# Attention, feed-forward and top-1 experts on one core: the gate logits of three token blocks on VectorE instead of TensorE, and two reorderings in block 0

## The chip, the core and the metric

The kernel runs on one core of a Trainium2 chip. The metric is the time of one execution on the device, in microseconds (us). Three executions of the kernel before took 570.47 to 570.69 us, median 570.53.

## What is computed

Three stages follow each other, over 1536 tokens with 512 features:

```python
# 1. attention: 2 sequences x 8 heads x 768 positions x 64; each position sees
#    the first 4 positions and the 128 latest
a = softmax(where(is_sink | in_window, q @ k.T / sqrt(D), -1e9)) ; attn = a @ v
x = attn as (1536, 512)
# 2. feed-forward, 512 -> 2048 -> 512; its weights come as 64-bit floats
h = x @ w_in ; g = maximum(0.01 * h, h) ; x = g @ w_out
# 3. eight experts, each token goes to one
logits = x @ w_gate                         # (1536, 8)
expert_idx = argmax(logits, axis=1) ; gate_w = softmax(logits)[expert_idx]
# a token keeps its place among the first 384 of its expert, in token order
y = maximum(x_of_expert @ w1[e], 0) @ w2[e] # 512 -> 1024 -> 512
out[i] = gate_w[i] * y[i] if kept else 0
```

The result is wanted in 32-bit precision.

## The kernel before

Large products are made from parts of 32-bit numbers: an operand is split in a *high* part (a cast, names `wh`, `xth`, `gp`) and a *low* part (the rest, `wl`, `xtl`), and a product is the sum of high x high, high x low and low x high.

**Blocks.** The feed-forward stage works on six blocks (0 to 5) of 256 tokens, each of two tiles of 128. For a block the 2048 hidden features are done in 16 *column tiles* f of 128: `first` (line 1084) makes `hps`, 12 products of 128x256 over the four slices k of the 512 features; `leak` (1102) applies the leaky maximum, with ScalarE at 1117 and VectorE's `max` at 1118; `split_g` (1121) makes the high half on ScalarE (1127) and the low half on GpSimd (1129); `second` (1132) adds the tile's part to the two outputs `y`, two column tiles later. Between these steps lie the steps of attention for a later block: transposes `qps`, VectorE's `qT` and `kTl` (586, 590), scores `sps` (617), the softmax (626 to 651), the outputs `ops` (713), and the low part of the attention output, `xtl`, in `pv_low` (728, VectorE at 732). Scores and other small TensorE results take turns in the same PSUM buffers.

**Block 0** is written out in `block0()` inside `build`. While it runs, VectorE makes 32-bit weights out of the 64-bit words, three operations of 128x512 for each piece: `low_word`, `sign` and `tail` (1017, 1021, 1027; tiles `word` and `cvt`). A first pass goes through `first` for f = 0 to 15, a second one through `second`. The first column tiles (five in the first pass, ten in the second) take their weights unsplit; from then on ScalarE casts `wh` (1045) and GpSimd subtracts `wl` (1046). The order of every engine is the order in which Python issues the work. A planner, `Pace`, keeps a time for TensorE and one for VectorE by assumed costs; whenever VectorE work is issued through `pace.vector`, `fill` first puts weight words in front of it for as long as the planner thinks that VectorE has time:

```python
    def vector(self, us, wait=0.0):
        self.fill()
        self.dve = max(self.dve, self.pe + wait) + us
```

After block 0 VectorE's order is left to the scheduler; the other engines keep the order written.

**Routing.** The last `second` of block j-1 falls in step 1 of block j's loop (a loop has 16 steps, one per column tile). ScalarE then copies `y` to a token tile (`evac`, 1224), and the routing steps of that block are put in a list, `routing`. After step i of the loop the next of them is issued if i is in `ROUTE`:

```python
ROUTE = (2, 4, 6, 9, 10, 11, 14)
                if routing and i in ROUTE:
                    routing.pop(0)()
```

The steps are: `transpose` (TensorE turns the token tile by eight transposes `xps`, line 1233; VectorE copies `x2T`, 1235), `parts` (sixteen small products `kls`, 1245, one ScalarE copy), `logits` (four products `lps`, 1258; VectorE finds the expert, 1265 to 1279), `place` (each token's row, 1293 to 1315) and two `scatter` (1322, an indirect DMA on GpSimd's queue that writes the tokens to their expert's rows). In block 4's loop `ex.rank` is put before the last of them; it sorts the experts by their counts. So the tokens of blocks 1, 2 and 3 are routed in the loops of blocks 2, 3 and 4. The experts' own products (`craw` and `cw`, 1472 and 1474, are their weights) come behind block 5. SP's queue carries the loads: attention's inputs (`natq`, 175), the weights and more.

Of the kernel before, what the change touches and what calls it, by code (L numbers as in the profile page):

```python
# [8 lines left out]
F32 = mybir.dt.float32  # L9
# [4 lines left out]
ALU = mybir.AluOpType  # L14
# [4 lines left out]
P = 128  # L19
# [14 lines left out]
PAIR = 2  # L34
# [12 lines left out]
AHEAD = (5, 10)  # L47
WORD_US = 0.6
PARTS_US = 2.0
ROUTE = (2, 4, 6, 9, 10, 11, 14)  # L50
HOLD, TAIL = 4, 1
QUIET = 2
# [376 lines left out]
class RingAttention(Attention):  # L429
# [298 lines left out]
    def pv_low(self, t, g):  # L728
        if (t, g) in self.lo:
            lo, hi, ps = self.lo.pop((t, g))  # L730
            self.pace.vector(0.4)
            self.nc.vector.tensor_tensor(out=lo, in0=ps, in1=hi.bitcast(F32), op=ALU.subtract)

    def pipeline(self, ts, n_first, first):
# [216 lines left out]
class FFN:  # L951
# [132 lines left out]
    def first(self, j, f):  # L1084
        nc, N = self.nc, self.N
        pool, tag = ("psy", "y1") if j == 0 and f % 2 else ("psh", "h")
        ps = self.p[pool].tile([P, 512], F32, tag=tag, name="hps")[:, 0:N]
        kc = lambda t: t.rearrange("p (k c) -> p k c", k=self.K)
        if self.in_parts(j, f, 0):
            wh, wl = map(kc, self.w[f][0])  # L1090
            xh, xl = [[x[:, k, :] for k in range(self.K)] for x in self.xt(j)] if j else \
                [[self.x0[k // 2][a][:, k % 2, :] for k in range(self.K)] for a in range(2)]
            mm = ((wh, xh), (wh, xl), (wl, xh))
        else:
            x = self.xt(j)[0]
            mm = ((kc(self.v[f][0]), [x[:, k, :] for k in range(self.K)]),)
        mm = [(w[:, k, :], x[k]) for k in range(self.K) for w, x in mm]
        for n, (w, x) in enumerate(mm):
            nc.tensor.matmul(ps, lhsT=w, rhs=x, start=(n == 0), stop=(n == len(mm) - 1))  # L1099
        self.g[j, f] = ps  # L1100
# [49 lines left out]
class Router:  # L1150


    def __init__(self, nc, tc, pools, A, capacity, ident):
        self.nc, self.tc, self.p, self.A = nc, tc, pools, A
        self.sent, self.both = [], ()
        self.ident = ident
        self.DM, self.E = A["moe2_w_gate"].shape
        self.NTOK = A["out"].shape[0]
        self.cap = max(0, min(int(capacity), self.NTOK))
        self.NU = -(-self.cap // P)  # L1160
        self.rows = self.NU * P
        self.K = self.DM // P
        self.OOB = 1 << 20
        self.KEEP = self.E // 2 - 1
        self.apart = self.NU > 1 and self.E > 1
        self.x2, self.xT, self.st = {}, {}, {}
        c = pools["const"]
        self.tiled = self.K * 32 <= P and self.E <= 32
        wg = c.tile([P, self.K, 32 if self.tiled else self.E], F32, name="wg")
        self.wgp, self.wg = wg, wg[:, :, 0:self.E]  # L1170
        if self.tiled:

            nc.gpsimd.memset(wg, 0.0)
            self.fold = c.tile([P, self.E], F32, name="fold")
            nc.gpsimd.memset(self.fold, 0.0)
            for k in range(self.K):
                nc.gpsimd.affine_select(out=self.fold, in_=self.fold, pattern=[[-1, self.E]],
                                        compare_op=ALU.not_equal, fill=1.0, base=-32 * k, channel_multiplier=1)
        self.lT = {}
        nc.sync.dma_start(out=self.wg, in_=A["moe2_w_gate"].rearrange("(k p) e -> p k e", p=P))  # L1180

        self.before = c.tile([P, P], BF16, name="before")
        nc.gpsimd.memset(self.before, 1.0)
        nc.gpsimd.affine_select(out=self.before, in_=self.before, pattern=[[1, P]], compare_op=ALU.is_gt, fill=0.0,
                                base=0, channel_multiplier=-1)
        self.ones = c.tile([P, P], BF16, name="ones")
        nc.gpsimd.memset(self.ones, 1.0)
        self.rev = c.tile([P, self.E], F32, name="rev")
        self.num = c.tile([P, self.E], F32, name="num")
        self.seat = c.tile([P, self.E], F32, name="seat")  # L1190

        seats, short = [0], list(range((self.E + 1) // 2, self.E))
        for e in range(1, (self.E + 1) // 2):
            seats += [e] + short[:1]
            del short[:1]
        seats += short
        for e in range(self.E):
            nc.gpsimd.memset(self.rev[:, e:e + 1], float(self.E - e))
            nc.gpsimd.memset(self.num[:, e:e + 1], float(e))
            nc.gpsimd.memset(self.seat[:, e:e + 1], float(seats[e]))  # L1200
        self.kept = c.tile([P, self.E], F32, name="kept")
        self.run = c.tile([P, self.E], F32, name="run")
        nc.gpsimd.memset(self.run, 0.0)
        self.tok = c.tile([P, self.NTOK // P], I32, name="tok")
        nc.gpsimd.iota(self.tok, pattern=[[P, self.NTOK // P]], base=0, channel_multiplier=1)

        self.places = pools["dram"].tile([max(1, self.rows * self.E), self.DM + 2], F32, name="places")
        self.queues = self.places[0:self.rows * self.E, :].rearrange("(e r) c -> e r c", e=self.E)
# [19 lines left out]
    def transpose(self, ts):  # L1228
        nc = self.nc
        for t in ts:  # L1230
# [4 lines left out]
            nc.vector.tensor_copy(xT, ps)  # L1235
            self.xT[t] = xT

    def parts(self, ts):

        nc = self.nc  # L1240
        ps = self.p["ps"].tile([32 * self.K, len(ts), P], F32, tag="att", name="kls")
        for n, t in enumerate(ts):
            xT = self.xT.pop(t)
            for k in range(self.K):
                nc.tensor.matmul(ps[32 * k:32 * k + 32, n, :], lhsT=self.wgp[:, k, :], rhs=xT[:, k, :],
                                 start=True, stop=True)
        lT = self.p["c"].tile([32 * self.K, len(ts), P], F32, tag="c", name="lT")
        nc.scalar.copy(lT, ps)
        self.lT[ts] = lT

    def logits(self, ts):
        nc, E, sm = self.nc, self.E, self.p["sm"]
        nt = len(ts)
        ps = self.p["ps"].tile([P, nt, E], F32, tag="att", name="lps")
        lT = self.lT.pop(ts, None)
        for n, t in enumerate(ts):
            if lT is not None:
                nc.tensor.matmul(ps[:, n, :], lhsT=lT[:, n, :], rhs=self.fold[0:32 * self.K, :], start=True, stop=True)
                continue
            xT = self.xT.pop(t)  # L1260
            for k in range(self.K):
                nc.tensor.matmul(ps[:, n, :], lhsT=xT[:, k, :], rhs=self.wg[:, k, :],
                                 start=(k == 0), stop=(k == self.K - 1))
# [4 lines left out]
        for n in range(nt):  # L1268
            nc.vector.scalar_tensor_tensor(out=sc[:, n, :], in0=ps[:, n, :], scalar=m[:, n:n + 1], in1=self.rev,
                                           op0=ALU.is_equal, op1=ALU.mult)  # L1270
# [7 lines left out]
                                op0=ALU.mult, op1=ALU.add)  # L1278
# [666 lines left out]
def build(tc, A, n_sink, window, capacity):  # L1945
    nc = tc.nc
# [3 lines left out]
    ring = RingAttention.fits(n_sink, window)  # L1950
    NTOK, DM = A["out"].shape
    N = FFN.N
    NB = NTOK // N
    TPB = N // P
    p = {}

    def pool(st, name, **kw):
        p[name] = st.enter_context(tc.tile_pool(name=name, **kw))

    with ExitStack() as es:  # L1960

        work, att, rawst, psy, psh, psc, pst = (ExitStack() for _ in range(7))
# [29 lines left out]
        steps, done = [], -1  # L1992
# [97 lines left out]
        rt = None  # L2090
# [13 lines left out]
        if not ring:  # L2104
            ex.PARTS -= FEWER

        pending, held, routing, splits = [], [], [], []
        n_ev = ffn.NF - ffn.CAP
        late = NB - 1

        def route(ts, ahead=False):
            return [lambda: rt.transpose(ts), *[lambda: rt.parts(ts)] * (ahead and rt.tiled), lambda: rt.logits(ts),
                    *[lambda: None] * (ahead and not rt.tiled), lambda: rt.place(ts),
                    *(lambda t=t: rt.scatter(t) for t in ts)]

        def split(n, f=-1, x=0):

# [4 lines left out]
        def second():  # L2122
# [23 lines left out]
            if last:  # L2146
                ts = tuple(range(j * TPB, (j + 1) * TPB))
                for t, y in zip(ts, ffn.y.pop(j)):
                    rt.evac(t, y)
                routing.extend(route(ts, True))  # L2150
                if j == late - 2 and rt.NU:
                    routing.insert(-1, ex.rank)

# [59 lines left out]
        pool(psh, "psh", bufs=2, side="right", space=PSUM)  # L2213
        rawst.close()
        pool(es, "rt", bufs=2)
        for j in range(1, NB):
            need_t = TPB * (j + 2) - 1
            count = next((n + 1 for n, x in enumerate(steps) if x[0] == need_t), len(steps))
            ndone = 0
            early = j == late and rt.NU  # L2220
            if j == late:
                att.close()
            if early:
                pool(es, "mx", bufs=1)
                ex.start_x()
            for i, f in enumerate(ffn.order(j)):
# [18 lines left out]
                    ndone += 1  # L2245
                split(SPLIT)
                some(clears, rate)
                if routing and i in ROUTE:
                    routing.pop(0)()
                if early:  # L2250
                    ex.room = min(ex.RAW + ex.PARTS, 6 + 4 * max(0, i - 1) - (0 if ring else FEWER))
# [84 lines left out]
```

## Time and profile before

| | |
|---|---|
| median of three executions | 570.53 us (570.47 to 570.69) |
| the profiled execution, its own time | 570.18 us |
| its span in the trace | 568.1 us, granted clock 0.998 |
| PE (TensorE) busy | 550.2 us, 97%, 3801 instructions |
| PEld (weight loads of TensorE, beside PE) | 472.4 us, 83% |
| DVE (VectorE) busy | 341.0 us, 60%, 829 instructions |
| ACT (ScalarE) busy | 291.6 us, 51% |
| POOL (GpSimd) busy | 186.4 us, 33% |
| DMA | 91.63 MB, mean 161 GB/s |

The page is of one profiled execution; 570.18 us is its whole time and 568.1 us the stretch from its first to its last recorded instruction. Busy time is an average over the whole program: block 0 ends at about 97 us, blocks 1 to 5 follow at some 60 us each, and the experts fill the rest. In a timeline row the first number is the start, the second how long it took, and brackets hold the idle time in front with what ended it.

### The profile page before, as it was taken

The numbers are of one execution on the slowest core, as the hardware profiler recorded it, in microseconds if no ns is written. First come the engines' busy times: TensorE is split into PE (matmuls) and PEld (weight loads), VectorE is DVE, ScalarE is ACT, GpSimd is POOL, SyncE is SP. The second block draws the span as 40 slices with busy tenths as digits, with TensorE's granted clock in tenths as the row PEclk, the third lists the DMA queues.
The fourth block names the chain that finished last, engine by engine and source line by source line (L and its number), as shares of the span: only waits on it lengthen the run. The fifth ranks groups of instructions, "written<-read, shape, count | busy, mean of one in ns | idle before, by whom it ended". The sixth has DMA issues, their size and how long they took to land.

```text
span 568.1 us, 11287 instructions
## 1 busy us (share of the span) xinstructions
PE 550.2 (97%) x3801; PEld 472.4 (83%) x3801; DVE 341.0 (60%) x829; ACT 291.6 (51%) x859; POOL 186.4 (33%) x338
## 2 busy tenths in 40 slices
PE   8988999999999999999999999999999999999994
PEld 7777657888898888888888888887899898988783
DVE  6999995766443533444444522575577666637992
ACT  6767646765445545444444433453444443526771
POOL 5567679623422243224332322241202011001120
PEclk9999999999999999999999999999999999999999
DMA  9979865999242023402230157562487676437930
GB/s 232 239 230 278 272 217 164 312 254 344 81 125 80 20 75 94 113 20 64 70 99 2 40 159 246 170 208 68 148 263 244 199 221 194 148 120 213 315 104 9
DMA packets 83557, 91.63 MB, mean 161 GB/s; under 512 B 42980, under 2 KB 51172, under 8 KB 83489
## 3 DMA queue, kind: packets, MB, share of 16 engines
q1 hardware_dynamic: 81504, 85.68, 50.3%
q0 software_dynamic: 1984, 5.13, 2.6%
q8 instruction: 32, 0.52, 0.4%
q14 instruction: 37, 0.29, 0.2%
HBM read 72.01 MB, written 20.09 MB: 162 GB/s over the span
## 4 chain that ended last, share of the span: by engine, by line
PE 75%; DVE 8%; issue 6%; DMA 5%; POOL 2%; ACT 2%; SPq 0%; POOLq 0%; DVEq 0%; ACTq 0%
PE hps L1099 21%; PE y L1147 21%; PE ph L1636 10%; PE py L1685 9%; PE ops L713 3%; PE sps L617 2%; DMA craw<-in_moe_w 2%; DMA out<-ys,gt 2%; DVE word L1017 2%; DVE word L1021 2%; PE pps L675 1%; PE qps L564 1%; DMA rawo<-in_moe_w_out 1%; DVE cvt L1027 1%; PE xps L1233 1%
## 5 line engine op out<-in xcount | busy, mean ns | idle before, releaser
L1147 PE MATMUL y<-wh,gp 128*128 128x512 f32 x344 | 126.7, 409 | 0.9 <-ACT gp L1127 0.7
L1129 POOL TENSOR_TENSOR gp<-g,gp 128x256 fp32r<-128x256 f32 x77 | 57.2, 743 | 179.9 <-ACT gp L1127 163.6
L1118 DVE TENSOR_TENSOR g<-hps,g 128x256 f32<-128x256 f32 x80 | 33.7, 422 | 103.6 <-ACT g L1117 101.5
L1099 PE MATMUL hps<-xth,wh 128*128 128x256 f32 x320 | 91.9, 287 | 0.4 <-DVE g L1118 0.4
L1099 PE MATMUL hps<-xtl,wh 128*128 128x256 f32 x320 | 90.2, 282 | 0.0
L1099 PE MATMUL hps<-xth,wl 128*128 128x256 f32 x320 | 89.9, 281 | 0.0
L1474 DVE TENSOR_TENSOR cw<-craw,cw 128x512 fp32r<-128x512 f32 x128 | 83.1, 693 | 10.3 <-ACT cw L1472 8.1
L1147 PEld LDWEIGHTS y<-wh,gp 128*128 128x128 f32 x344 | 64.5, 188 | 16.0 <-ACT gp L1127 1.1
L1472 ACT CAST cw<-craw 128x512 fp32r<-128x512 f32 x112 | 63.3, 621 | 23.7 <-PE py L1685 23.0
L1117 ACT ACTIVATE g<-hps 128x256 f32<-128x256 f32 x80 | 30.6, 382 | 84.6 <-PE hps L1099 80.0
L1147 PE MATMUL y<-wl,gp 128*128 128x512 f32 x172 | 67.6, 393 | 0.0
L1685 PE MATMUL py<-cw,ht 128*128 128x512 f32 x264 | 64.1, 398 | 0.2 <-DVE ht L1673 0.2
L1099 PEld LDWEIGHTS hps<-xth,wh 128*128 128x128 f32 x320 | 60.3, 188 | 4.5 <-DVE g L1118 1.4
L1099 PEld LDWEIGHTS hps<-xtl,wh 128*128 128x128 f32 x320 | 60.2, 188 | 2.1
L1099 PEld LDWEIGHTS hps<-xth,wl 128*128 128x128 f32 x320 | 60.6, 189 | 0.0
L1685 PEld LDWEIGHTS py<-cw,ht 128*128 128x128 f32 x264 | 48.9, 188 | 11.8 <-DVE ht L1673 1.0
L1636 PE MATMUL ph<-xt,cw 128*128 128x256 f32 (+2 forms) x444 | 57.7, 290 | 0.1
L1636 PEld LDWEIGHTS ph<-xt,cw 128*128 128x128 f32 x444 | 56.5, 189 | 0.5 <-issue 0.3
L1694 POOL DMA_INDIRECT out<-ys,gt x11 | 11.1, 1007 | 112.8 <-DVE ys L1693 101.8
L1127 ACT CAST gp<-g 128x256 fp32r<-128x256 f32 x80 | 32.9, 411 | 21.6 <-DVE g L1118 20.2
L640 ACT ACTIVATE pm<-pm,mx 128x132 f32<-128x132 f32 (+1 forms) x80 | 31.9, 402 | 10.3 <-DVE mx L632 10.3
L1147 PEld LDWEIGHTS y<-wl,gp 128*128 128x128 f32 x172 | 32.5, 189 | 4.4 <-POOL wl L1046 0.3
(255 smaller groups left out, 993.1 us busy)
## 6 DMA issues: line engine op xcount, KB each, us to landing
craw<-in_moe_w SPq DMA_DIRECT2D x128, 256.0 KB
rawi<-in_moe_w_in SPq DMA_DIRECT2D x16, 512.0 KB
rawo<-in_moe_w_out SPq DMA_DIRECT2D x16, 512.0 KB
places<-zero SPq DMA_DIRECT2D x24, 257.0 KB
wh<-wscr SPq DMA_DIRECT2D x16, 256.0 KB
wl<-wscr SPq DMA_DIRECT2D x16, 256.0 KB
xg<-places SPq DMA_DIRECT2D x12, 257.0 KB
natv<-in_v SPq DMA_DIRECT2D x12, 256.0 KB
```

The lines of the kernel that those rows point to most:

```text
L640: self.nc.scalar.activation(a, a, AF.Exp, bias=mx[:, pr, e:e + 1], accum_out=su[:, pr, e, 0:1])
L713: nc.tensor.matmul(ps[64 * e:64 * e + 64, pr, :], lhsT=l, rhs=r, start=(x == 0 and not (late and pr)), stop=(x == len(mm[0]) - 1 and not l ...
L1099: nc.tensor.matmul(ps, lhsT=w, rhs=x, start=(n == 0), stop=(n == len(mm) - 1))
L1117: nc.scalar.activation(g, ps, AF.Copy, scale=0.01)
L1118: nc.vector.tensor_tensor(out=g, in0=ps, in1=g, op=ALU.max)
L1127: nc.scalar.copy(gp[:, 0], g)
L1129: eng.tensor_tensor(out=gp[:, 1], in0=g, in1=gp[:, 0].bitcast(F32), op=ALU.subtract)
L1147: nc.tensor.matmul(y, lhsT=l, rhs=r, start=(start and n == 0), stop=(stop and n == len(mm) - 1))
L1472: nc.scalar.copy(h, t)
L1474: eng.tensor_tensor(out=l, in0=t, in1=h.bitcast(F32), op=ALU.subtract)
L1636: nc.tensor.matmul(self.ph[f][:, sl], lhsT=self.w[e, "a", h, k][w][:, f * P:(f + 1) * P], rhs=self.xt[:, a, k, sl], start=(m == 0), stop=( ...
L1685: nc.tensor.matmul(self.py[n], lhsT=x, rhs=w, start=(h == 0 and f == 0 and m == 0), stop=(h == self.NH - 1 and f == self.HF - 1 and m == 2))
```

## The change

1. **Logits of blocks 1, 2 and 3 on VectorE.** At the start of block 2's loop SP issues a load of `rows_of`, the 512x8 gate weights copied to each of the 128 partitions (16 KB each, 2.1 MB). For each token tile and each expert one `scalar_tensor_tensor` multiplies the tile (128x512) by that expert's 512 weights, which lie 8 words apart, and sums each row into the logit: 16 such products for a block. Two are issued after each of eight steps (a list `beside`), 1 to 8. Then `logits` (without its TensorE part), `place` and the two scatters come in steps 9, 10, 11 and 12, `AFTER` in the place of `ROUTE`; with `ex.rank` in block 4's loop it is 12 and 13 for the last two. The transposes, `parts` and the `lps` products of these three blocks are gone. Blocks 0, 4 and 5 are routed as before.
2. **Low weights last in block 0.** In `first` of block 0 the 12 products run high x high for all k, high weight x low token for all k, then low weight x high token, and no longer k by k.
3. **`pv_low` without words in front.** It adds its cost to the planner's time by itself and does not call `fill`.

```diff
+AFTER = range(9, 16)
 ROUTE = (2, 4, 6, 9, 10, 11, 14)
...
     def pv_low(self, t, g):
         if (t, g) in self.lo:
             lo, hi, ps = self.lo.pop((t, g))
-            self.pace.vector(0.4)
+            self.pace.dve = max(self.pace.dve, self.pace.pe) + 0.4
             self.nc.vector.tensor_tensor(out=lo, in0=ps, in1=hi.bitcast(F32), op=ALU.subtract)
...
-        mm = [(w[:, k, :], x[k]) for k in range(self.K) for w, x in mm]
+        mm = [(w[:, k, :], x[k]) for w, x in mm for k in range(self.K)] if j == 0 else \
+            [(w[:, k, :], x[k]) for k in range(self.K) for w, x in mm]
...
+    def start_rows(self):
+
+        self.rows_of = self.p["wgb"].tile([P, self.DM, self.E], F32, name="rows_of")
+        src = self.A["moe2_w_gate"].rearrange("(o d) e -> o (d e)", o=1)
+        self.nc.sync.dma_start(out=self.rows_of.rearrange("p d e -> p (d e)"),
+                               in_=src.to_broadcast([P, self.DM * self.E]))
+
+    def products(self, ts, n, es):
+
+        nc, DM = self.nc, self.DM
+        if ts not in self.lg:
+            self.lg[ts] = self.p["sm"].tile([P, len(ts), self.E], F32, tag="rsc", name="rlg")
+        junk = self.p["c"].tile([P, DM], F32, tag="c", name="junk")
+        for e in es:
+            nc.vector.scalar_tensor_tensor(out=junk, in0=self.x2[ts[n]][:, 0:DM], scalar=1.0,
+                                           in1=self.rows_of[:, :, e], op0=ALU.mult, op1=ALU.mult,
+                                           accum_out=self.lg[ts][:, n, e:e + 1])
...
-        ps = self.p["ps"].tile([P, nt, E], F32, tag="att", name="lps")
+        ps = self.lg.pop(ts, None)
+        done = ps is not None
+        if not done:
+            ps = self.p["ps"].tile([P, nt, E], F32, tag="att", name="lps")
...
-        for n, t in enumerate(ts):
+        for n, t in enumerate(() if done else ts):
...
         def route(ts, ahead=False):
+            if ahead and rt.rows_of is not None and len(ts) == 2:
+                es = list(range(rt.E))
+                beside.extend(lambda n=n, e=e: rt.products(ts, n, es[e:e + PAIR])
+                              for n in range(len(ts)) for e in range(0, rt.E, PAIR))
+                return [lambda: rt.logits(ts), lambda: rt.place(ts), *(lambda t=t: rt.scatter(t) for t in ts)]
...
+        def late_route(ts):
+            rt.rows_of = None
+            return route(ts, True)
...
-                routing.extend(route(ts, True))
+                routing.extend(route(ts, True) if j < late - 1 else late_route(ts))
...
+            if j == 2 < late and ring and rt.tiled and TPB == 2:
+                pool(wgb, "wgb", bufs=1)
+                rt.start_rows()
...
             if j == late:
+                rt.rows_of = None
+                wgb.close()
                 att.close()
...
-                if routing and i in ROUTE:
+                if beside:
+                    beside.pop(0)()
+                elif routing and i in (ROUTE if rt.rows_of is None else AFTER):
                     routing.pop(0)()
```

How VectorE's order changes in steps 1 to 3 of block 2's loop, where the tokens of block 1 are routed (`g` is the leak's maximum, `x_2526` a token tile, `junk` the products themselves, `rlg` their sums). Before:

```order
L1118 TENSOR_TENSOR g<-hps,g 128x256
L648 TENSOR_REDUCE ri<-su_134 128x4
L649 RECIPROCAL ri<-ri 128x4
L1118 TENSOR_TENSOR g<-hps,g 128x256
L586 SCALAR_TENSOR_TENSOR qT<-qps,qT 128x256
L590 TENSOR_TENSOR kTl_130<-qps,kTh_129 128x2x128
L1235 COPY x2T<-xps 128x512 x2
L1118 TENSOR_TENSOR g<-hps,g 128x256
L732 TENSOR_TENSOR xtl<-ops,xth 128x2x128
L533 TENSOR_TENSOR vh<-vsraw,vh 32x256
```

And with the change:

```order
L1120 TENSOR_TENSOR g<-hps,g 128x256
L1255 SCALAR_TENSOR_TENSOR junk,rlg<-x_2526,rows_of 128x512 x2
L649 TENSOR_REDUCE ri<-su_134 128x4
L650 RECIPROCAL ri<-ri 128x4
L1120 TENSOR_TENSOR g<-hps,g 128x256
L587 SCALAR_TENSOR_TENSOR qT<-qps,qT 128x256
L591 TENSOR_TENSOR kTl_130<-qps,kTh_129 128x2x128
L1255 SCALAR_TENSOR_TENSOR junk,rlg<-x_2526,rows_of 128x512
L1120 TENSOR_TENSOR g<-hps,g 128x256
L1255 SCALAR_TENSOR_TENSOR junk,rlg<-x_2526,rows_of 128x512
L733 TENSOR_TENSOR xtl<-ops,xth 128x2x128
L534 TENSOR_TENSOR vh<-vsraw,vh 32x256
```

The products stand between the maxima of the leak and the attention steps, and in front of `xtl`; the two copies of `x2T` are gone.

TensorE in block 0, the sixth column tile, the first whose weights are split (`x0h` and `x0l` are the parts of the tokens). Before:

```order
L1099 MATMUL hps<-xth,cvt 128x256 x8
L1099 MATMUL hps<-x0h,wh 128x256
L1099 MATMUL hps<-x0l,wh 128x256
L1099 MATMUL hps<-x0h,wl 128x256
L1099 MATMUL hps<-x0h,wh 128x256
```

and so on, four times three products, one k after the other.

And with the change:

```order
L1101 MATMUL hps<-xth,cvt 128x256 x8
L1101 MATMUL hps<-x0h,wh 128x256 x4
L1101 MATMUL hps<-x0l,wh 128x256 x4
L1101 MATMUL hps<-x0h,wl 128x256 x4
L565 MATMUL qps<-ident,natq 128x128 x2
```

The first use of `wl` moves from the third place of twelve to the ninth.

VectorE in block 0, around `pv_low` (`xtl`). Before:

```order
L590 TENSOR_TENSOR kTl_130<-qps,kTh_129 128x2x128
L1017 TENSOR_SCALAR word<-rawo 128x512 x2
L732 TENSOR_TENSOR xtl<-ops,xth 128x2x128
L1021 SCALAR_TENSOR_TENSOR word<-rawo,word 128x512
L627 COPY_PREDICATED pm<-sel,sps 128x128 x4
L632 TENSOR_REDUCE mx<-pm 128x4
```

And with the change:

```order
L591 TENSOR_TENSOR kTl_130<-qps,kTh_129 128x2x128
L1018 TENSOR_SCALAR word<-rawo 128x512 x2
L733 TENSOR_TENSOR xtl<-ops,xth 128x2x128
L1022 SCALAR_TENSOR_TENSOR word<-rawo,word 128x512
L628 COPY_PREDICATED pm<-sel,sps 128x128 x4
L633 TENSOR_REDUCE mx<-pm 128x4
```

Nothing moved here but the line numbers, and the rest of VectorE's rows in block 0 are the same too. On GpSimd's queue the scatters move, and SP has one row more, the load of `rows_of` between the loads of `natq` and `natk` and that of `natv`.

## Rows read from the trace of the kernel before

**Rows 1.** Stage table: stretch, length; busy us of engines; PEclk, DMA, GB/s.

```profile
97.00:156.00 59.00, 59.00 (x462) 51.88 (x461) 34.60 (x95) 34.35 (x117) 26.61 (x42) 1.00 0.87 255
165.20:195.70 30.50, 30.50 (x236) 26.45 (x234) 14.19 (x45) 16.59 (x61) 8.79 (x15) 1.00 0.24 62
```

**Rows 2.** Waits (us, times, longest): TensorE, whole; VectorE, 26 to 82.6.

```profile
PE hps L1099 <- POOL wl L1046: 3.6, 5, 0.9
...
DVE word L1017 <- DMA rawo<-in_moe_w_out: 0.5, 1, 0.5
```

**Rows 3.** Timelines near the end of block 0: start, us, engine, line.

```profile
71.98 0.69 DVE L1017 TENSOR_SCALAR word<-rawo 128x512 int32<-128x512 int32 x1 [0.54 <-DMA rawo<-in_moe_w_out]
...
82.73 1.07 POOL L651 TENSOR_TENSOR pm<-pm,ri 128x528 f32<-128x528 f32 x1 [2.48 <-DVE ri L649]
...
95.20 0.74 POOL L1129 TENSOR_TENSOR gp<-gr,gp 128x256 fp32r<-128x256 f32 x1
...
95.99 0.73 PE L1147 MATMUL y<-wh,gp 128*128 128x512 f32 x2 [0.19 <-POOL gp L1129]
```

**Rows 4.** Timeline of TensorE in block 2's loop.

```profile
168.26 0.39 PE L1147 MATMUL y<-wh,gp 128*128 128x512 f32 x1
168.49 1.04 PE L1233 MATMUL xps<-ident,x 128*128 128x128 f32 x8
169.49 0.28 PE L1099 MATMUL hps<-xtl,wh 128*128 128x256 f32 x1
...
172.73 0.39 PE L1147 MATMUL y<-wh,gp 128*128 128x512 f32 x1
173.07 0.28 PE L1099 MATMUL hps<-xtl,wh 128*128 128x256 f32 x1
...
176.66 0.39 PE L1147 MATMUL y<-wh,gp 128*128 128x512 f32 x1
176.98 0.64 PE L1245 MATMUL kls<-x2T,wg 128*32 128x128 f32 x16
177.77 0.28 PE L1099 MATMUL hps<-xtl,wh 128*128 128x256 f32 x1
...
183.93 0.39 PE L1147 MATMUL y<-wh,gp 128*128 128x512 f32 x1
184.16 0.51 PE L1258 MATMUL lps<-fold,lT 128*128 128x8 f32 x4
184.72 0.28 PE L1099 MATMUL hps<-xtl,wh 128*128 128x256 f32 x1
```

**Rows 5.** Groups by shape: busy us, mean ns of one, idle before.

```profile
L1235 DVE COPY x2T<-xps 128x512 f32<-128x512 f32 x12 | 7.8, 685 | 4.2 <-PE xps L1233 4.2
L1046 DVE TENSOR_TENSOR wl<-cvt,wh 128x512 fp32r<-128x512 f32 x10 | 8.5, 846 | 3.8 <-ACT wh L1045 3.7
L1338 DVE TENSOR_REDUCE kept<-sel 128x8 f32<-128x24 f32 x1 | 0.2, 181 | 0.0
L1306 DVE TENSOR_REDUCE rpp<-rpos 128x2 f32<-128x16 f32 x5 | 0.8, 169 | 0.0
L1354 DVE TENSOR_REDUCE rank<-gt 128x8 f32<-128x64 f32 x2 | 0.4, 210 | 0.0
L640 ACT ACTIVATION_READ_ACCUMULATOR pm<-pm,mx 128x1 f32 x80 | 15.4, 192 | 0.0
L1021 DVE SCALAR_TENSOR_TENSOR cvt<-rawo,cvt 128x512 int32<-128x512 int32 x1 | 1.4, 1410 | 0.0
```

**Rows 6.** Timelines of VectorE and TensorE, middle of block 2's loop.

```profile
187.22 0.42 DVE L732 TENSOR_TENSOR xtl<-ops,xth 128x256 fp32r<-128x256 f32 x1
189.71 0.40 PE L617 MATMUL sps<-kTh,qT 64*128 64x264 f32 x2
```

**Rows 7.** Timelines of SP's queue and ScalarE.

```profile
148.54 0.52 SPq L175 DMA_DIRECT2D natq<-in_q  x1
...
164.85 1.17 ACT L1224 COPY x<-y 128x512 f32<-128x512 f32 x2
```

**Rows 8.** One tile's instructions: min/median/max ns, first and last start.

```profile
L1472 ACT CAST cw<-craw x112: 608/621/635, 356.6 to 555.5; 128x512 fp32r<-128x512 f32 x112
```

More of the change, by code (lines that the diff above doesn't have):

```diff
@@ L1180, in __init__ @@
         nc.sync.dma_start(out=self.wg, in_=A["moe2_w_gate"].rearrange("(k p) e -> p k e", p=P))
+        self.rows_of, self.lg = None, {}
         self.before = c.tile([P, P], BF16, name="before")
@@ L2105, in build @@
             ex.PARTS -= FEWER
-        pending, held, routing, splits = [], [], [], []
+        pending, held, routing, splits, beside = [], [], [], [], []
         n_ev = ffn.NF - ffn.CAP
@@ L2215, in build @@
         pool(es, "rt", bufs=2)
+        wgb = ExitStack()
         for j in range(1, NB):
+            if j == 2 < late and ring and rt.tiled and TPB == 2:
+                pool(wgb, "wgb", bufs=1)
+                rt.start_rows()
             need_t = TPB * (j + 2) - 1
```

## The prediction, made before the changed kernel ran

> **What bounds the kernel now.** I read the stage table first, then TensorE's waits, then the timelines. From block 1 on TensorE is the bound: it is busy for 59.00 of 59.00 us in block 1 and for 30.50 of 30.50 us in the first half of block 2, at a granted clock of 1.00, while VectorE works 14.19 us of the same 30.50 [rows 1]. There, work taken off TensorE is time, and VectorE has room.
>
> Block 0 is different. TensorE's longest list of waits is there: 3.6 us in five waits for a low weight part [rows 2]. Yet TensorE does not set that block's end. Near it, TensorE stops for a low half from GpSimd, at 95.99, right behind the `gp` that ran 95.20 to 95.94. GpSimd had been working through its queue since 82.73, which it began after an idle 2.48 us, released by `ri` of VectorE. VectorE in turn works through weight words up to that `ri` with one stop, 0.54 us before 71.98, for a DMA [rows 3]; its list of waits from 26 us on has nothing else [rows 2]. So block 0 ends when VectorE's words and GpSimd's splits are through, and a TensorE that is early merely waits at 95.99 instead.
>
> **The change, part by part.** *Removed from TensorE, three times.* I take the distance from the last `y` to the second `hps` behind it. Undisturbed it is 172.73 to 173.07, 0.34. With the eight transposes between it is 168.26 to 169.49, 1.23, so they cost 0.89. With the sixteen small `kls` products it is 176.66 to 177.77, 1.11: 0.77. With the four `lps` it is 183.93 to 184.72, 0.79: 0.45 [rows 4]. Together 2.11 us; all of it is on the path, since TensorE has no gap around it. Three blocks: 3 x 2.11 = 6.3 us gained. ScalarE loses one small copy per block and is not the bound.
>
> *Added to VectorE.* Per block 16 products of 128x512 whose two inputs lie in SBUF, one read in steps of 8 words, each with a sum. No row shows this instruction, so I build its price. The nearest plain form, one operation over 128x512, is 685 ns. The group `wl` of VectorE, with both inputs in SBUF and GpSimd working beside it, takes 846 on average: 0.16 for that company. Steps of 8 words occur in one small row: `kept<-sel`, 24 elements, 181 ns, where a line through 169 for 16 elements and 210 for 64 gives 176. The 5 ns over 24 elements make 0.2 ns each, so 0.10 us for 512. Reading out a sum is a row of 192 ns on ScalarE; VectorE shows none, so I take half, 0.10. That makes 0.69 + 0.16 + 0.10 + 0.10 = 1.05 us. The ends are 0.69, nothing added, and 1.41, the longest single row of this size with two SBUF inputs [rows 5]. I stay near the 846 row, because it has the same two kinds of input, in the same stage.
>
> *Does it fit?* The products are due in steps 1 to 9. TensorE's stretch shrinks to 30.50 - 2.11 = 28.4 us. VectorE's other work there is 14.19 [rows 1] less two copies of 685 ns [rows 5], 12.8. That leaves 15.6 us of room. A late VectorE first meets TensorE at the scores: `xtl` ends at 187.64, the scores that want its PSUM buffer start at 189.71, 2.07 us of slack [rows 6]. (15.6 + 2.07) / 16 = 1.10 us per product is the point from which TensorE waits. At 1.05 nothing shows; beyond 1.10 each tenth costs 1.6 us per block, 4.8 in all, and at 1.10 + 2.11 / 16 = 1.23 the gain is gone. The leak's `max`, which stands between the products on VectorE, has its reader two steps on, further off than the scores. GpSimd's low halves may wait for a product, and their readers are as far off.
>
> *The 2.1 MB of weight rows.* SP issues them right behind the load at 148.54. At the 255 GB/s of block 1 [rows 1] they take 8.2 us and are there at about 158. The first product needs its token tile, which ScalarE copies from 164.85 [rows 7]. Seven microseconds of cover: nothing.
>
> *Moved.* Logits go from steps 4 and 6 to 9, places from 9 to 10, the scatters from steps 10 and 14 to 11 and 12 (13 in block 4): the same instructions on VectorE, TensorE and the GpSimd queue, three steps before the next block wants their buffers. The expert ranking goes from step 11 to 12, one step later; SP waits for it before it asks for expert weights, whose first conversion is at 356.6 [rows 8], half a block on. Nothing.
>
> *Block 0.* With the low weights last, eight of twelve products run before the low part is needed, so most of the 3.6 us goes from that place and comes back at 95.99. The cover is GpSimd's queue; if it went, up to 3.6 us would be gained. I take 0. The edit of `pv_low` changes only the planner's sum: VectorE's order in block 0, shown above, is the same row for row, so no word moves, and it is worth 0 by any account.
>
> **Sum.** The profiled execution took 570.18 us, and 570.18 - 6.3 = 563.9. The median is 0.35 above it, so I say 564.2.
>
> **Rivals.** *VectorE becomes the bound, and the kernel slower.* Mechanism: the step of 8 words slows each product, the backlog reaches `xtl`, and the scores wait for their PSUM buffer in blocks 2, 3 and 4. It decides from 1.23 us per product. At the upper end, 1.41, the wait is 16 x (1.41 - 1.10) = 5.0 us per block, 15 in all, and 570.5 + 15 - 6.3 = 579.2. For it speaks that VectorE is filled to the brim in these steps; against it the 181 ns row, where full one-element steps cost little. [...]
>
> *Block 0 pays as well.* If GpSimd's chain were released by TensorE somewhere, 3.6 us more would go: 560.6. Against it: VectorE's one stop in front of that `ri` is for a DMA and not for TensorE [rows 2].
>
> *The weight rows come late.* The first product would hold VectorE, and behind it the `max` of step 2. The seven microseconds speak against it; price some 5 us once, 569.
>
> **Numbers.** About 0.2% (1.1 us) can be told from no change here. The forecast, 563 to 566, has 0.61. Between 1.10 and 1.20 us per product, or with late weight rows, part of the gain is left, 566 to 569.4: 0.10. Block 0 paying: 0.04. A product near 1.23, within 0.2%: 0.07. VectorE the bound: 0.18, about half of it above 577. So faster 0.75, same 0.07, slower 0.18. The range is 562.5 to 577: it leaves out 0.04 below and about 0.09 above.
>
> **What the changed profile would show.** Right: products of about 1.05 us; no `xps`, `kls` and `lps` in the loops of blocks 2 to 4; each of those blocks some 2 us shorter with TensorE still busy throughout; the five waits for `wl` in block 0 gone, and block 1 starting where it did, at about 97. Wrong: waits of `sps` or `hps` on VectorE in blocks 2 to 4, with products above 1.2 us; or block 1 starting 2 us earlier.

## The result, and the profile after

| | before | changed |
|---|---|---|
| median of five executions | 570.51 us (570.26 to 570.69) | 564.75 us (563.96 to 565.62) |
| ratio | | 0.9901, 95% interval 0.9888 to 0.9915 |
| the profiled execution, its span | 570.18, 568.1 us | 564.84, 563.1 us |

564.75 stands against a predicted 564.2, in a range of 562.5 to 577. Some executions run in a slower state, and the medians and ratios here and below leave them out: one of run 8 (653.87 us) and one of the kernel before beside it (1074.87 us). The page of the changed kernel, busy time by engine:

```profile
PE 544.9 (97%) x3717; PEld 467.7 (83%) x3717; DVE 394.8 (70%) x919; ACT 291.2 (52%) x856; POOL 209.2 (37%) x338
```

TensorE lost 84 instructions and 5.3 us of work; VectorE gained 54 us, and GpSimd, which got nothing new to do, 23 us. The stage table of the changed kernel, for block 1 and for the first half of block 2 (columns as in [rows 1]):

```profile
97.00:156.00 59.00, 59.00 (x464) 51.93 (x463) 34.77 (x95) 34.24 (x116) 26.53 (x42) 1.00 0.93 287
...
165.20:193.60 28.40, 28.40 (x205) 25.09 (x204) 27.94 (x61) 13.30 (x46) 15.17 (x14) 1.00 0.25 66
```

TensorE still works without a gap, but in block 2's half VectorE now works 27.94 of 28.40 us and GpSimd 15.17 instead of 8.79 [rows 1]. Why, the groups of the changed kernel tell (busy us, mean ns of one, idle before):

```profile
L1131 POOL TENSOR_TENSOR gp<-g,gp 128x256 fp32r<-128x256 f32 x77 | 66.4, 862 | 150.7 <-ACT gp L1129 129.8 <-PE hps L1101 8.8 <-PE y L1149 7.1
L1255 DVE SCALAR_TENSOR_TENSOR junk<-x,rows_of 128x512 f32<-128x512 f32 x48 | 62.9, 1309 | 1.2 <-ACT x L1227 1.0
L1255 DVE DVE_READ_ACCUMULATOR junk<-x,rows_of 128x1 f32 x48 | 4.2, 87 | 0.0
```

A product takes 1.31 us on average, not the 1.05 of the prediction, and the low halves of GpSimd take 862 ns on average where they took 743. One place shows how the two engines meet. The timelines of VectorE and GpSimd in block 2:

```profile
169.05 1.64 DVE L1255 SCALAR_TENSOR_TENSOR junk<-x,rows_of 128x512 f32<-128x512 f32 x1
170.63 0.08 DVE L1255 DVE_READ_ACCUMULATOR junk<-x,rows_of 128x1 f32 x1
170.63 0.41 DVE L1120 TENSOR_TENSOR g<-hps,g 128x256 f32<-128x256 f32 x1
170.97 1.71 DVE L1255 SCALAR_TENSOR_TENSOR junk<-x,rows_of 128x512 f32<-128x512 f32 x1
...
169.00 0.74 POOL L1131 TENSOR_TENSOR gp<-g,gp 128x256 fp32r<-128x256 f32 x1 [2.19 <-ACT gp L1129]
169.68 1.92 POOL L652 TENSOR_TENSOR pm<-pm,ri 128x512 f32<-128x512 f32 x1
171.57 1.73 POOL L1131 TENSOR_TENSOR gp<-g,gp 128x256 fp32r<-128x256 f32 x1
```

A product and a GpSimd instruction take turns here: whichever begins while the other is under way ends late. The product of 169.05 begins while a low half still has 0.69 us to go, and ends 0.95 us after that low half. The normalization begins at 169.68, within the product, and ends 0.91 us after it; its row is 1.92 us, where the same one took 1.04 in the kernel before. The next product and the next low half go the same way.

All 48 products follow this. 29 of them had no GpSimd instruction with more than a quarter of a microsecond to go when they began; they took 1.09 to 1.25 us, 1.17 in the mean, even where a GpSimd instruction began inside them. The other 19 took 1.32 to 1.72, 1.53 in the mean, and ended 0.95 to 1.07 us after the GpSimd instruction that they met. In return, 14 low halves that began within a product end 0.60 to 0.63 us after it. So part of VectorE's and GpSimd's busy time in the stage table is waiting for each other.

The read-out of the sum has a row of 0.08 us, but the next instruction starts together with it, at 170.63: it costs nothing.

Where the gain arises, the start of ScalarE's first leak in each block shows, against the kernel before. I put the experiments beside it; a block's gain is the difference of two rows. All numbers are differences of starts in two traces, in us.

| first leak of | before, start | changed | products only | low last only | one later | turned copies | four more | block 1 too | loads earlier |
|---|---|---|---|---|---|---|---|---|---|
| block 1 | 98.75 | -0.15 | +0.29 | +0.42 | -0.05 | +0.09 | +0.55 | -0.01 | +0.03 |
| block 2 | 159.83 | -0.17 | +0.23 | +0.35 | -0.07 | +1.61 | +0.52 | +5.68 | 0.00 |
| block 3 | 219.53 | -1.97 | -1.54 | +0.35 | -2.09 | -0.44 | +3.59 | +3.85 | -2.04 |
| block 4 | 280.66 | -3.67 | -3.24 | +0.35 | -3.82 | -2.52 | +6.51 | +2.14 | -4.08 |
| block 5 | 339.72 | -5.52 | -5.02 | +0.35 | -5.60 | -4.65 | +11.47 | +0.35 | -6.21 |

Two runs are not in the table: the changed kernel again (run 9) stands at -0.10, -0.08, -1.89, -3.59 and -5.34, and run 3 at -0.68 and then, behind a long stop in block 1, at +27.56, +25.52, +23.47 and +21.35.

So block 0 gives 0.15 us, which is within what these rows scatter from profile to profile (the kernels with the edit of `first` stand between -0.68 and +0.55), and blocks 2, 3 and 4 give 1.80, 1.70 and 1.85. Inside block 2 TensorE's own rows show the three removals. These are the second `hps` behind each of the three places, to be held against those at 169.49, 177.77 and 184.72 in [rows 4]:

```profile
168.43 0.28 PE L1101 MATMUL hps<-xtl,wh 128*128 128x256 f32 x1
...
175.97 0.28 PE L1101 MATMUL hps<-xtl,wh 128*128 128x256 f32 x1
...
182.49 0.28 PE L1101 MATMUL hps<-xtl,wh 128*128 128x256 f32 x1
```

TensorE's lead grows from 0.17 at the start of the block to 1.06 where the transposes were, to 1.80 where `kls` was and to 2.23 where `lps` was. That is 2.06 us gained, of which some 0.25 is lost again before the block ends; blocks 3 and 4 gain 2.04 and 2.07 by the same reading and lose 0.34 and 0.22.

**Where 0.2 to 0.35 us per block come back.** In blocks 3 and 4 it is at the place that the prediction named, the scores. The timelines of VectorE and TensorE in block 3 of the changed kernel:

```profile
247.10 0.41 DVE L733 TENSOR_TENSOR xtl<-ops,xth 128x256 fp32r<-128x256 f32 x1
...
246.82 0.40 PE L618 MATMUL sps<-kTh,qT 64*128 64x264 f32 x2
247.05 0.29 PE L618 MATMUL sps<-kTl,qT 64*128 64x264 f32 x2
247.18 0.78 PE L618 MATMUL sps<-kTh,qT 64*128 64x264 f32 x4
247.57 0.51 PE L618 MATMUL sps<-kTl,qT 64*128 64x264 f32 x2
```

`xtl` ends at 247.51; the third group of scores, the last of which wants its buffer, is stretched to 0.78 where the same one takes 0.40 in block 2, and the weight loads' list of waits has it as well, `PEld sps <- DVE xtl`, 0.2 us. In block 2 the loss is at `place`, in step 10: its list of weight loads' waits (190 to 200) reads

```profile
PEld L1317 <- DVE roh L1298: 0.5, 1, 0.5
```

TensorE wants the one-hot rows `roh` of `logits`, which VectorE finishes late behind its products. Another 0.5 us goes among the experts' first products: the lead is 5.52 at block 5 and 5.0 at the end of the span. VectorE stands 0.94 us in front of a `cw` at 406.60 there (0.53 before), and TensorE then waits 0.34 for `ht` behind it. What holds that `cw` was not tried.

**Block 0.** TensorE's waits from 24 to 97 us, changed kernel:

```profile
PE hps L1101 <- ACT wh L1046: 1.9, 3, 0.9
PE sps L618 <- DVE xtl L733: 1.1, 2, 0.8
PE hps L1101 <- POOL wl L1047: 0.5, 3, 0.2
PE pps L676 <- DVE pm L628: 0.4, 1, 0.4
PE y L1149 <- POOL gp L1131: 0.2, 1, 0.2
```

The sum is 4.1 us. Before, it was 4.1 too: 3.6 for `wl` [rows 2], 0.3 for one `xtl` and 0.2 for the low half at the end. The waits for `wl` shrank from 3.6 to 0.5, and waits for `wh`, for `xtl` and for the softmax came, all of results that VectorE makes or that are made from its words; the wait of 0.19 for `gp` stands at 95.84 instead of 95.99 [rows 3].

### The profile page after: what moved, and what is told of

It is laid out like the page before. It is cut to its first block, busy times and chain, and to the rows that moved or that the text cites. A ratio compares the mean times of both kernels' runs of the same rounds, so it can differ in the third digit from the quotient of the medians.

```text
span 563.1 us, 11193 instructions
## 1 busy us (share of the span) xinstructions
PE 544.9 (97%) x3717; PEld 467.7 (83%) x3717; DVE 394.8 (70%) x919; ACT 291.2 (52%) x856; POOL 209.2 (37%) x338
## 5 line engine op out<-in xcount | busy, mean ns | idle before, releaser
L1131 POOL TENSOR_TENSOR gp<-g,gp 128x256 fp32r<-128x256 f32 x77 | 66.4, 862 | 150.7 <-ACT gp L1129 129.8
L1255 DVE SCALAR_TENSOR_TENSOR junk<-x,rows_of 128x512 f32<-128x512 f32 x48 | 62.9, 1309 | 1.2 <-ACT x L1227 1.0
```

What stands on the lines that cost most here:

```text
L1131: eng.tensor_tensor(out=gp[:, 1], in0=g, in1=gp[:, 0].bitcast(F32), op=ALU.subtract)
L1255: nc.vector.scalar_tensor_tensor(out=junk, in0=self.x2[ts[n]][:, 0:DM], scalar=1.0, in1=self.rows_of[:, :, e], op0=ALU.mult, op1=ALU.mult, ...
```

## The experiments

The theory, after these rows: the gain is TensorE's 2.05 us per block, a product is long because of its step, VectorE is full to within what its readers bear, and block 0's two edits are worth nothing. The rivals: block 0 carries part of the gain; GpSimd's company makes the product long; VectorE could be later still at no cost.

**1. Products only.** The edits of block 0 are undone.

```diff
-        mm = [(w[:, k, :], x[k]) for w, x in mm for k in range(self.K)] if j == 0 else \
-            [(w[:, k, :], x[k]) for k in range(self.K) for w, x in mm]
+        mm = [(w[:, k, :], x[k]) for k in range(self.K) for w, x in mm]
...
-            self.pace.dve = max(self.pace.dve, self.pace.pe) + 0.4
+            self.pace.vector(0.4)
```

> The products of blocks 1 to 3 on VectorE alone; block 0 in its old order, pv_low with its words in front. Theory (TensorE loses 2.05 us per block, 0.25 to 0.35 of it comes back where place waits for a late VectorE, block 0's edits are worth 0.15): 564.9 us, block 1's first leak on ScalarE at 98.75 as before the change, the next blocks 1.8 us earlier each. Rival (the edits of block 0 carry a part of the gain): 566 to 568 us.

Measured: 565.16 us (563.83 to 565.78), ratio 0.9904 [0.9891, 0.9917]. Blocks 2 to 4 give 1.77, 1.70 and 1.78. The products carry the gain; block 1 starts 0.44 us later than in the changed kernel, but this scatters, as the next run shows, which starts it at +0.42 with the edit in.

**2. Low weights last only**, on the kernel before, with the first two lines of the diff above the other way round.

> Block 0's low weights last, alone. Theory (block 0 ends when VectorE's words and GpSimd's splits are through): 570.35 us, 0.15 under the kernel before; TensorE's waits for wl nearly gone, waits for wh and for other results of VectorE in their place. Rival (the 3.6 us of waits were on the path): 567 to 569.5 us.

Measured: 570.47 us, ratio 1.0002 [0.9993, 1.0010]. TensorE's waits, 24 to 97 us:

```profile
PE hps L1100 <- ACT wh L1045: 1.9, 3, 0.9
PE sps L617 <- DVE xtl L732: 1.7, 2, 0.9
PE hps L1100 <- POOL wl L1046: 0.5, 3, 0.2
```

Waiting of 3.6 us for `wl` turned into 1.9 for `wh` and 1.7 for `xtl`, with 0.5 left for `wl`: worth 0. The rival on block 0 falls. `pv_low` was not run alone; its program has the same rows in the same order.

**3. Weights side by side, turned by a DMA.**

```diff
-        self.rows_of = self.p["wgb"].tile([P, self.DM, self.E], F32, name="rows_of")
+        self.rows_of = self.p["wgb"].tile([P, self.E, self.DM], F32, name="rows_of")
...
+            self.nc.sync.dma_start(out=self.turned[:, :], in_=self.A["moe2_w_gate"].rearrange("d e -> e d"))
...
-                                           in1=self.rows_of[:, :, e], op0=ALU.mult, op1=ALU.mult,
+                                           in1=self.rows_of[:, e, :], op0=ALU.mult, op1=ALU.mult,
```

> The changed kernel with the gate weights turned once in DRAM, so that an expert's 512 weights lie side by side in SBUF and a product reads without steps. Theory (the step of 8 words makes up most of a product's 1.31 us): a product takes 0.70 to 0.75 us where GpSimd is idle and 0.85 to 0.9 where it works, VectorE falls from 27.9 to about 20 us of 28.4 in block 2's first half, the wait of place goes, 563.9 us. Rival (company of GpSimd or the reading out of the sum makes it long): products stay above 1.1 us, time as the changed kernel, 564.75.

Measured: 591.97 us (591.24 to 598.02), ratio 1.0399. The step was right, the way to it was not. The products (shortest, median and longest in ns), a store of SP's queue, and the waits of ScalarE and TensorE in block 1:

```profile
L1260 DVE SCALAR_TENSOR_TENSOR junk<-x,rows_of x48: 675/685/1159, 193.0 to 336.4; 128x512 f32<-128x512 f32 x48
...
99.99 28.27 SPq L1057 DMA_DIRECT2D wscr<-wh  x1
...
ACT wh L1046 <- DMA wscr<-wh: 30.0, 1, 30.0
...
PE y L1149 <- ACT wh L1046: 24.6, 1, 24.6
```

A product without steps takes 685 ns in the median, exactly what a copy of 128x512 takes [rows 5]. While GpSimd is idle a product takes 0.68 us without steps (7 of them) and 1.19 with (10, in the changed kernel). So the step of 8 words costs about 0.50 us, two inputs in SBUF and the sum nothing. GpSimd's company is again a matter of turns: 33 products that did not meet a GpSimd instruction with more than a quarter of a microsecond to go took 0.68 to 0.74, the other 15 took 0.82 to 1.16 and each ended 0.55 us after that instruction. Over all 48 this adds 0.08 us to a product in the mean here, and 0.14 in the changed kernel. But the little DMA that turns the weights, 4096 words one by one (the run has 4104 DMA packets more than the changed kernel), keeps SP's queue: the store behind it has a row of 28.27 us, ScalarE's cast waits 30.0 us for a buffer that this store reads, and block 1 stands still for 24.6 us. Blocks 2 to 4 give 2.04, 2.05 and 2.12 here.

**4. One step later:** `AFTER = range(10, 16)`.

> The changed kernel with logits, place and scatters one step later. Theory (in step 10 TensorE waits 0.25 to 0.35 us for the one-hot rows of a VectorE that is behind with its products): that wait goes in three blocks, 563.9 us. Rival (the loss of block 2 to 4 lies elsewhere, or VectorE is as late a step on): 564.75 us.

Measured: 565.14 us (564.46 to 566.07), ratio 0.9914; the time shows no gain. The theory was right for block 2 alone: it gives 2.02, the wait for `roh` is gone. Blocks 3 and 4 give 1.73 and 1.78, as before, because theirs is the wait at the scores. I had read one block and written of three.

**5. Weights side by side, turned by ScalarE.** In place of the one load, in block 1's loop from step 2 on, one piece k of 64 features per step, copied two steps behind its load:

```diff
+            raw[k] = self.p["c"].tile([P, n, self.E], F32, tag="c", name="raw_of")
+            self.nc.sync.dma_start(out=raw[k].rearrange("p d e -> p (d e)"),
+                                   in_=src[:, k * self.DM:(k + 1) * self.DM].to_broadcast([P, self.DM]))
...
+            self.nc.scalar.copy(self.side[:, :, k * n:(k + 1) * n], raw.pop(k).rearrange("p d e -> p e d"))
```

> The changed kernel with an expert's 512 weights side by side in SBUF, as in the run before on the step, but turned there: in block 1's loop SP loads the copied gate weights in eight pieces of 64 features, and ScalarE writes each piece in order of experts. Theory (with the step 0.3 us per block come back at the scores or at place, since VectorE is full): products 0.69 us alone and 0.82 beside GpSimd, no wait of TensorE for VectorE in blocks 2 to 4, 2.05 us less per block instead of 1.80, 0.8 us under the changed kernel: 564.0 us. Rival (the eight copies and loads cost block 1 as much as they bring, or VectorE's lateness costs nothing): 564.9 us or more.

Measured: 565.45 us (564.76 to 567.87), ratio 0.9917. Blocks 2 to 4 give 2.05, 2.08 and 2.13, as expected; block 1 loses 1.52. ScalarE's waits from 97 to 160 us:

```profile
ACT rows_of L1254 <- DMA raw_of<-in_moe_w_gate: 7.9, 6, 2.7
```

It stands before loads that have not landed, with the leaks of TensorE's results queued behind it. Theory and rival were both right, each in its block.

**6. Four more products per block**, the first product of every second pair done twice.

```diff
-        for e in es:
+        for e in es + es[:1] * (es[0] % 4 == 0):
```

> The changed kernel with four of the sixteen products of a block done a second time, into the same place: 20 products per block. Theory (at 16 the low part of the attention output is already as late as the scores can bear, so whatever is put in front of it is TensorE's loss): three of the four stand in front of it, 3 x 1.36 = 4.1 us per block, 12 us in all, 577 us, and the waits are at the scores of blocks 2 to 4. Rival (VectorE may lag further, its readers are far off): 565 to 567 us.

Measured: 581.21 us, ratio 1.0176 [1.0158, 1.0194]. TensorE's waits from 97 to 345 us, its rows at the scores of blocks 3 and 4 and at the `y` that ends the next column tile, and a row of the stage table (columns as in [rows 1]):

```profile
PE sps L618 <- DVE xtl L733: 6.9, 3, 2.8
PE pps L1317 <- DVE roh L1298: 1.5, 2, 0.8
PE kps L680 <- DVE pm L628: 1.4, 2, 0.7
...
256.99 0.39 PE L618 MATMUL sps<-kTh,qT 64*128 64x264 f32 x1 [2.81 <-DVE xtl L733]
...
260.92 0.48 PE L1149 MATMUL y<-wh,gp 128*128 128x512 f32 x1
...
320.97 0.59 PE L618 MATMUL sps<-kTh,qT 64*128 64x264 f32 x1 [2.82 <-DVE xtl L733]
...
327.81 0.47 PE L1149 MATMUL y<-wh,gp 128*128 128x512 f32 x1
...
321.00:327.00 6.00, 6.00 (x22) 5.18 (x23) 5.97 (x13) 1.10 (x4) 2.26 (x2) 0.50 0.01 3
```

Against the changed kernel blocks 2, 3 and 4 lose 4.87, 4.62 and 6.81 us, 16.3 in all. Four products more are some 5.2 us of VectorE at 1.31 each, 15.7 in three blocks. Not all of the loss is VectorE's: behind the stop in block 4 the granted clock falls to 0.50 while TensorE works without a gap, and from those scores to the `y` it takes 6.84 us where the same work takes 3.93 in block 3, at a granted clock of 1.00. That is 2.9 us; why a stop of the same length in block 3 was not followed by a fall isn't shown. Without it 13.4 us are lost for 15.7 added: a microsecond more on VectorE is most of a microsecond of TensorE. VectorE is full at 16; the rival falls. My 12 us at the scores were not what came: 6.9 us are stops there, some 4.2 are stops at `place`, at the softmax and at low halves and maxima, 2.9 are the clock, and 2.3 are in no listed stop.

**7. Block 1 too.** The rows are loaded at the start of block 1's loop (`if j == 1` for `if j == 2`), so the tokens of block 0 are routed by products as well.

> The changed kernel with the weight rows loaded one block earlier and the products also for the tokens of block 0, in block 1's loop. Theory (VectorE works 34.6 of 59.0 us there, with ten low weight parts of its own; 16 products of 1.36 us in the first half do not fit): TensorE is relieved of 2.05 us and gives back 3 to 6 us at the scores or at the low weight parts: 566 to 569 us. Rival (it fits as in the other blocks): 563.0 us.

Measured: 571.13 us, ratio 1.0005 [0.9992, 1.0018]. Block 1 is 5.69 us longer although TensorE has 2.05 less to do there, so 7.7 are given back where I expected 3 to 6; the other blocks give 1.83, 1.71 and 1.79. TensorE's rows, and a row of the stage table:

```profile
116.44 0.39 PE L618 MATMUL sps<-kTh,qT 64*128 64x264 f32 x1 [2.33 <-DVE xtl L733]
134.13 0.39 PE L618 MATMUL sps<-kTh,qT 64*128 64x264 f32 x1 [2.38 <-DVE xtl L733]
...
136.00:139.00 3.00, 3.00 (x14) 2.89 (x13) 3.00 (x9) 0.93 (x2) 1.12 (x1) 0.50 1.06 340
```

Some 1.3 of the 7.7 us are again the clock, which falls to 0.50 behind the second stop: from those scores to the `y` that ends the next column tile it is 5.48 us, and 4.15 behind the first stop. One block where VectorE has other work takes back all that three gave. Here the prediction's rival decides: VectorE bounds the block.

**8. Turned by ScalarE, loads earlier.** As 5, with the loads in steps 0 to 7 and each copy six steps behind.

> As the run with turned copies, but the eight loads are issued in steps 0 to 7 of block 1's loop and each copy six steps behind its load. Theory (block 1 lost 1.5 us there because ScalarE stood 7.9 us before loads that had not landed, and its leaks and casts behind it): ScalarE waits under 1 us for these loads, block 1 loses at most 0.3 us, blocks 2 to 4 keep their 2.05 to 2.1 us each, 6.2 in all, and the kernel is 0.5 to 0.9 us under the changed one on the same chip. Rival (the copies' own 9.7 us on ScalarE, or the 2.1 MB beside block 1's stores, cost the time): block 1 loses 1 us or more again, no gain over the changed kernel.

**9. The changed kernel again**, on the same chip.

> The changed kernel as it is, for comparison on the same chip: 564.5 to 565.3 us, or 5.3 to 5.9 us under the kernel before.

Measured: 564.01 us for 8 (three executions, 563.93 to 564.04), ratio 0.9893 [0.9873, 0.9913], and 564.79 us (563.58 to 565.14) for 9, ratio 0.9899 [0.9882, 0.9917]. In times the two cannot be told apart; the traces tell them apart block by block. In 8 block 1 loses nothing (+0.03 to 0.00), though ScalarE works 42.77 of 59.00 us there and waits for no load, and blocks 2 to 4 give 2.04, 2.04 and 2.13. Its products, and its row of the stage table for block 2's half:

```profile
L1265 DVE SCALAR_TENSOR_TENSOR junk<-x,rows_of 128x512 f32<-128x512 f32 x48 | 37.0, 772 | 1.2 <-ACT x L1227 1.0
...
165.20:193.60 28.40, 28.40 (x204) 25.06 (x202) 23.26 (x69) 15.21 (x53) 11.13 (x15) 1.00 0.25 66
```

It is 0.7 us ahead of the changed kernel at block 5, and 1.1 at the end of the span (562.0 against 563.1): the version to keep, if its few more lines are worth that.

## Why the prediction was right, point by point

*The bound and the removals: right.* 0.89, 0.77 and 0.45 were read off the rows; 0.89, 0.74 and 0.43 came back. All of it was on the path; with faster products (8) it stays there, 6.21 us of the 6.3.

*The price of a product: wrong.* The step that failed is "5 ns over 24 elements make 0.2 ns each, so 0.10 us for 512". The step of 8 words costs 0.50 us, five times that. At the measured rate of about 1 ns the 24 elements would have cost some 23 ns instead of 5; why that row shows so little was not tried. Not every step costs: the words of block 0 are read in steps of 2 words, and their row of 0.69 us [rows 3] is that of a copy, 685 ns [rows 5]. The other terms were sound or small: base 0.69 (0.685), company 0.16 (0.14 in the mean, but all of it in the 19 products that met a GpSimd instruction), read-out 0.10 (0, as it runs under the next instruction). The sum 1.05 was 1.31.

*The point from which TensorE waits: wrong too, in the other direction.* I divided the room by 16 products and got 1.10. In VectorE's timeline of the changed kernel only 12 of them (block 2) or 13 (blocks 3 and 4) stand in front of that `xtl`, the rest behind it, with readers of their own further off. By my own division 17.7 / 13 is 1.36. That is too kind, since part of that room lies behind `xtl` too: at 1.31 TensorE already loses 0.2 to 0.35 us. The slack was read short as well: not the first of the twelve score products wants the buffer but the eighth, before which runs 6 and 7 stop, and in the kernel before it starts at 190.19 and not at 189.71. Had 1.10 been true, 1.31 would have cost 3.4 us per block and left a slower kernel, 574.3. So the price was too low by 0.26 and the limit too low by about as much: the two errors nearly cancel, and that the time came out right is luck. My margin was not right: I wrote that nothing would show, and run 6 shows that VectorE stands at the brim.

*What the profile would show: partly wrong.* The blocks got shorter by nearly 2 us with TensorE busy throughout, as written. But products above 1.2 us with a wait of `sps` for VectorE stand among my signs of being wrong, and both came: 1.31 us, and the `xtl` that stretches the scores of blocks 3 and 4. A reader of the time alone would not have seen it.

*The rival: right in kind and place, wrong in its condition.* It was to decide from 1.23 us per product; at 1.31 it took back 0.2 to 0.35 us per block and not the whole gain. A backlog at `xtl` with the scores waiting does decide once four products are added (6) or another block is included (7).

*Block 0 and `pv_low`: right in the sum.* "Most of the 3.6 us goes from that place and comes back": it does (2), but not at the 95.99 I named, where the wait is 0.19 as before. It comes back earlier, at `wh`, at `xtl` and at the softmax.

*The 2.1 MB, the moved steps: right.* SP issues the load at 148.33 and it lands 9.6 us later; the first product starts at 165.29, when its token tile is there. (In blocks 2 and 3 the second scatter came from step 11 and not from 14, as block 4's does; nothing hangs on it.) What I had not seen: `logits` right behind the last product makes `place` wait in block 2, and a step later it does not (4).

## What to carry to other kernels

Work taken from the bounding engine is worth its own rows, as long as the engine that takes it over is not late for its readers; so count which of the added instructions stand in front of the first reader, not all of them. A price for reading in steps must come from a row as long as the one it is for: a row of 24 elements gave 0.2 ns each here, one of 512 about 1 ns. VectorE and GpSimd, taking turns, lengthened each other's rows here, and the mean of a product, 1.31 us, hid two prices, 1.53 where it met a GpSimd instruction and 1.17 elsewhere: look at what the other engine was doing when an instruction began. And VectorE at 98% in a stage (27.94 of 28.40 us) was a second bound here: 15.7 us more of its work cost 13.4 us of time (6), before the clock.

## What was not expected

GpSimd gets slower without getting work: its low halves went from 743 to 862 ns in the mean, and to 810 with products that have no steps (8). It is the other side of the turns: a low half that begins within a product ends some 0.6 us after it with either kind of product, so the shorter product makes the shorter wait.

The clock fell to 0.50 behind stops of TensorE in runs 6 and 7. In run 3 the stage table shows it at a long stop. Columns as in [rows 1]:

```profile
102.00:126.00 24.00, 20.13 (x162) 17.51 (x159) 9.05 (x21) 8.58 (x28) 6.40 (x11) 1.00 0.81 1
126.00:128.00 2.00, 0.00 (x0) 0.00 (x0) 0.00 (x0) 0.00 (x0) 0.00 (x0) 0.52 0.49 0
128.00:130.00 2.00, 0.00 (x0) 0.00 (x0) 0.00 (x0) 0.00 (x0) 0.00 (x0) 0.50 1.15 145
```

The granted clock is 1.00 up to 126 us, and 0.52 and then 0.50 while TensorE stands still afterwards; the first product behind the stop has a row of 0.79 us, where one takes 0.40 elsewhere. Block 2 starts 27.6 us later than before for a stop of 24.6.

The DMA share of those 24 us is 0.81 at 1 GB/s: 4096 words moved one by one kept the engines nearly as busy as 255 GB/s did in block 1 of the kernel before, 0.87 [rows 1].
